# Six of twelve score tiles a pair transposed by PE, and a plan that holds an engine for an operation's time less its overlap with the next

## The chip, the cores and the metric

The kernel runs on one core of one Trainium2 chip. The metric is the device time of one execution in microseconds, as the median of several runs.

## The reference

Attention over buckets, then two feed-forward layers, all in float32. Both batches (2) and heads (8) have 768 tokens of 64 numbers.

```python
q_bucket = sum over 6 bits of ((q @ proj) > 0) * 2**bit      # k_bucket alike
scores = where(q_bucket[:, None] == k_bucket[None, :], q @ k.T / 8, -1e9)
attn = exp(scores - max); attn = attn / (sum + 1e-9)
x = (attn @ v), heads side by side                           # 1536 x 512
h = x @ w_in;  g = maximum(0.01 * h, h);            x = g @ w_out    # 512 -> 2048 -> 512
h = x @ w_in2; g = max(h, 0) + alpha * min(h, 0);   out = g @ w_out2
```

The weights come as float64 and are turned to float32 on the chip by integer operations.

## The kernel before, in words

**Attention.** The 16 heads go in eight pairs (two heads of one batch, index `i`; the head is `j`). Of a pair there are twelve score tiles of 128 query rows by 768 keys: two halves `f` of the rows, in each six tiles `m`, whose row block `t` and head `j` stand in `TILES`. `score` (from L694) makes one: PE multiplies (L710) into one of two PSUM tiles of the ring `s_ps`; DVE copies it to one of five buffers of the ring `s` and takes the row minimum (L717); ACT takes the exponential with its row sum (L720). Then the tile must be turned over, keys onto partitions, for the product with v. There are two ways, and `HI_ON` and `LO_ON` (for the last pair `HI_LAST` and `LO_LAST`) say for each of the twelve tiles which is taken:

- `T`: PE transposes the float32 tile in two groups of three (L736), each through the one PSUM bank of the ring `p_ps`, and ACT copies each group to `pt` (L741, `FP` = 0 leaves ACT alone).
- else: the tile is split in two float16 halves. With `P` in `LO_ON`, POOL scales it (L413, called at L752) and subtracts for the low half (L416); with `D`, DVE makes the low half in one operation (L760). The high half is a cast (L754) by ACT, or also by POOL where the plan may choose: before, for the `D` tiles alone; with `FH` = 1 for both. When both heads of a row block are there, one DMA transpose from SP's queue turns them over (L766).

`pv` multiplies with v for a half: six steps of PE, in each six float16 products over the row blocks that were split (L807) and two float32 products for each block that came by `T` (L816; each stands in the trace as two records). `kept` counts the split blocks of a half. Then DVE multiplies by the reciprocal sum (L823). For the next pair k and q are loaded, split (L416 on POOL, `split_qk`), turned over (L539) and their bucket bits made (L582, L591).

**Feed-forward.** Both layers run over four groups of 512 hidden columns and the two batches. `convert` (from L965) turns a float64 weight piece to float32 by five operations (ACT L993, DVE L995, L999, L1002, L1005) and to a scaled float16 pair; the common scale of a group comes out of `power` (from L924), with a PE product with ones (L950) that spreads a maximum over the partitions, in a PSUM bank of `b_banks`, and a DVE read of it (L954). Every product is three float16 products (L1164 to L1166). `leaky` makes the activation, `y_group` (from L1267) the second product and its sum (L1298).

**The order of the work.** Nothing is ordered by hand: each step is an operation of `Plan`, with one or more `ways` (engine, cost in us, for DVE whether it needs the port that it shares with POOL in the model, and for a DMA its time on the queue), a `claim` that orders the ring buffers, and a `turn` that orders operations that are ready at one time. `Plan.first` makes a list schedule, `late` and `early` push it back and forth (`PASSES`, for six values of `PATIENCE`), and the order that ends first by the costs is written out for each engine. `Lines` holds each engine from an operation's start to its cost's end; `hop` is the delay between engines, 0 on the same one. In this model a DMA transpose takes SP for 3.7 and the DMA line for 4.0 us.

Of the kernel before, what the change touches and what calls it, by code (L numbers as in the profile page):

```python
# [27 lines left out]
F64_MAX = 122879.9921875  # L28

TILES = ((0, 0), (2, 0), (0, 1), (1, 0), (2, 1), (1, 1))  # L30
HI_ON = "ATPATPATPATA"
LO_ON = "P-DP-DP-DP-D"

HI_LAST = "ATPATPATATTT"
LO_LAST = "P-DP-DP-D---"
SB = 5
FT, FP, FR, FH, FV, FB = 0, 0, 1, 0, 0, 0


HOP, HOP_PE, LANDING = 0.12, 0.29, 1.6  # L40
PATIENCE, PASSES = (0.05, 0.1, 0.15, 0.2, 0.25, 0.3), 7


LEAN_V, LEAN_X, LEAN_W = 0.0,0.0,0.0

X_LEAD, CONV = 30, (2, 5, 19, 6)
START, XAT = 10.0, (1, 9)

# [48 lines left out]
    __slots__ = ("ways", "claim", "reads", "writes", "deps", "left", "users", "n", "start", "done", "way", "turn", "lean")  # L97


def hop(one, other):  # L100

    return 0.0 if one[0] == other[0] != "SP" else HOP_PE if one[0] == "PE" else HOP


class Line:
# [25 lines left out]
class Lines(dict):  # L131
# [9 lines left out]
    def soonest(self, op, last=False):  # L141

        best = None
        for k, way in enumerate(op.ways):
            eng, dur, port, _ = way
            at = 0.0
            for u, full in op.deps.items():
                at = max(at, u.done + hop(u.ways[u.way], way) if full else u.start)
            lines, x = self.of(way), 0.0
            if last:  # L150
                at = max([at] + [line.ends[-1] for line in lines if line.ends])
            else:
                while (then := max(line.early(at, dur) for line in lines)) > at + 1e-9:
                    at = then
            done = at + dur
            if eng == "SP":
                x = at + dur / 2
                x = max([x] + self["DMA"].ends[-1:]) if last else self["DMA"].early(x, port)
                done = x + port + LANDING
            cost = done - (op.lean if eng == "POOL" else 0.0)  # L160
            if best is None or cost < best[0]:
                best = cost, (at, done, x, k)
        return best[1]

    def latest(self, way, start, done):
        eng, dur, port, _ = way
        if eng == "SP":
            x = self["DMA"].late(done - LANDING, port)
            return self["SP"].late(min(start, x - dur / 2) + dur, dur), x + port + LANDING, x
        at, lines = min(start, done - dur), self.of(way)  # L170
        while (then := min(line.late(at + dur, dur) for line in lines)) < at - 1e-9:
            at = then
        return at, at + dur, 0.0

    def put(self, way, at, x):
        for line in self.of(way):
            line.put(at, way[1])
        if way[0] == "SP":
            self["DMA"].put(x, way[2])

# [125 lines left out]
def lsh_attention_ffn_kernel(  # L306
# [13 lines left out]
    nc = tc.nc  # L320
    B, H, S, D = q.shape
# [15 lines left out]
    NP = len(pairs)  # L337
    N = 12 * NP

    ctx.enter_context(tc.manual_schedule())  # L340
    plan = Plan()
# [55 lines left out]
    def vec(dur, fn, port=False):  # L397
        return "DVE", dur, port, fn
# [4 lines left out]
    def gps(dur, fn):  # L403
        return "POOL", dur, 0, fn
# [270 lines left out]
        )  # L675

    def engines(i):
        return (HI_ON, LO_ON) if i < NP - 1 else (HI_LAST, LO_LAST)

    def kept(i, f):  # L680

# [233 lines left out]
    def bank(ring):  # L915
        return Bank(ring.new([128, 1, HALF], F32, "h"), 0)
# [7 lines left out]
    def power(claim, cols_, most, most_use, scale_, scale_use, extra=None, reads=(), writes=(), wide=False, to=2.0**13):  # L924

        dg_ = bt_r.new([128, S], F32, "dg")
        dg = lambda: dg_.t.bitcast(F32R)[:, 0:128]
        mx = mx_r.new([128, 1], F32, "mx")
        ps = b_banks.take() if claim >= N + 2 else bank(t_ps)
        buf, n = cols_  # L930

        def diag():
            nc.vector.tensor_reduce(out=mx.t, in_=buf.t[:, 0:n], axis=AX.X, op=ALU.max)
            if not wide:
                nc.vector.tensor_single_scalar(
                    mx.t.bitcast(I32), mx.t.bitcast(I32), EXPONENT, op=ALU.bitwise_and
                )
                return
            low, high = buf.t[:, 0:1].bitcast(I32), mx.t.bitcast(I32)
            nc.vector.tensor_scalar(  # L940
                out=low, in0=high, scalar1=3, scalar2=0x3F800000, op0=ALU.logical_shift_left,
                op1=ALU.bitwise_and,
            )
            nc.vector.scalar_tensor_tensor(
                out=high, in0=high, scalar=0x40000000, in1=low, op0=ALU.bitwise_and, op1=ALU.bitwise_or
            )

        plan.add(claim, vec(0.5 if wide else 0.35, diag), [buf], [mx, buf] if wide else [mx])
        plan.add(claim, diagonal(dg, mx), [mx, ident], [dg_])
        plan.add(claim, pe(0.2, lambda: nc.tensor.matmul(  # L950
            ps.ap(128), lhsT=ones.t, rhs=dg(), start=True, stop=True)), [dg_, ones], [ps.use()])

        def scales():
            nc.vector.tensor_reduce(out=most(), in_=ps.ap(128), axis=AX.X, op=ALU.max)  # L954
            nc.vector.tensor_scalar_max(most(), most(), V_MIN)
            nc.vector.tensor_single_scalar(
                scale_().bitcast(I32), most().bitcast(I32), EXPONENT, op=ALU.bitwise_xor
            )
            nc.vector.tensor_scalar_mul(scale_(), scale_(), to)  # L959
            if extra:  # L960
                extra()

        plan.add(claim, vec(0.95 if extra else 0.8, scales), [ps.use(), *reads], [most_use, scale_use, *writes])

    def convert(n, claim, step, early=None):  # L965

        l, fq, nm = groups[n]
        mw = mw_r.new([128, FQ], F32, "mw")
# [2 lines left out]
        for k in range(FQ // per):  # L971
# [5 lines left out]
            for a, one in enumerate(each):  # L977
# [14 lines left out]
            w = per * DM  # L992
            plan.add(first, act(0.16 + w * 0.00098, lambda m=m, high=high: nc.scalar.activation(  # L993
                out=m.ap(F32), in_=high().bitcast(F32), func=AF.Abs)), [r.use()], [m.use()], turn=now)
            plan.add(first, vec(0.24 + w * 0.00052, lambda m=m, k=k: nc.vector.tensor_scalar(  # L995
                out=m.ap(F32), in0=m.ap(F32), scalar1=F64_MAX, scalar2=F64_MIN, op0=ALU.min,
                op1=ALU.max, accum_out=mw.t[:, k:k + 1]), True),
                [m.use()], [m.use(), col(mw, k)], turn=now)
            plan.add(first, vec(0.18 + w * 0.00052, lambda m=m: nc.vector.tensor_scalar(  # L999
                out=m.ap(I32), in0=m.ap(I32), scalar1=3, scalar2=0x3FFFFFFF,  # L1000
                op0=ALU.logical_shift_left, op1=ALU.bitwise_and), True), [m.use()], [m.use()], turn=now)
            plan.add(first, vec(0.19 + w * 0.00104, lambda m=m, low=low: nc.vector.scalar_tensor_tensor(  # L1002
                out=low(), in0=low(), scalar=29, in1=m.ap(I32), op0=ALU.logical_shift_right,
                op1=ALU.bitwise_or), True), [m.use(), r.use()], [r.use()], turn=now)
            plan.add(first, vec(0.19 + w * 0.00104, lambda low=low, high=high: nc.vector.scalar_tensor_tensor(  # L1005
                out=low(), in0=high(), scalar=-0x40000000, in1=low(), op0=ALU.bitwise_and,
                op1=ALU.bitwise_or), True), [r.use()], [r.use()], turn=now)

# [37 lines left out]
        for p in range(0, FQ, 2):  # L1046
# [16 lines left out]
            for out_, x, y, op, to, frm in (  # L1063
                (s1, a21, a22, ALU.add, r1, r2), (s3, a11, a21, ALU.subtract, r2, r1),
                (s2, s1, a11, ALU.subtract, r1, r1), (s4, a12, s2, ALU.subtract, r2, r1),
            ):
                def add(out_=out_, x=x, y=y, op=op, eng=None):
                    eng.tensor_tensor(out=out_(), in0=x(), in1=y(), op=op)
                plan.add(claim, [
                    vec(0.37, lambda add=add: add(eng=nc.vector), True),  # L1070
                    gps(0.7, lambda add=add: add(eng=nc.gpsimd))], [r1.use(), r2.use()], [to.use()])
            halves(claim, wide, lambda r1=r1: r1.ap(F32).rearrange("p (d two) -> p two d", two=2),
                   [r1.use()], c, c_use, 2)
            halves(claim, thin, lambda r2=r2: r2.ap(F32).rearrange("p (d two) -> p two d", two=2)[:, :, DM // 2:],
# [70 lines left out]
    def x_sum(b, nm, claim, turn):  # L1145
        (x, xu), (y, yu) = (x_part(b, a) for a in {
            "T3": ("B22", "B12"), "T1": ("B12", "B11"), "T2": ("B22", "B11"), "T4": ("B21", "B11")}[nm])
        o, ou = (y, yu) if nm == "T2" else (x, xu)
        op = ALU.add if nm == "T2" else ALU.subtract
        plan.add(claim, [vec(0.95, lambda: nc.vector.tensor_tensor(out=o(), in0=x(), in1=y(), op=op), True),  # L1150
                         gps(1.9, lambda: nc.gpsimd.tensor_tensor(out=o(), in0=x(), in1=y(), op=op))],
                 [xu, yu], [ou], turn)

# [29 lines left out]
    def leaky(u, f, n, claim, src, src_use, own=None):  # L1183
# [7 lines left out]
        else:  # L1191
            plan.add(claim, act(0.58, lambda: nc.scalar.activation(
                out=g.ap(F32), in_=src(), func=AF.Copy, scale=low_by.t[:, f:f + 1])),
                [src_use, low_by], [g.use()])
            plan.add(claim, vec(0.56, lambda: nc.vector.scalar_tensor_tensor(  # L1195
                out=g.ap(F32), in0=src(), scalar=high_by.t[:, f:f + 1], in1=g.ap(F32),
                op0=ALU.mult, op1=ALU.max), own is not None), [src_use, g.use(), high_by], [g.use()])
        plan.add(claim, act(0.51, lambda: nc.scalar.copy(out=gh.ap(), in_=g.ap(F32))),  # L1198
# [221 lines left out]
```

## Time and profile before

| | before |
|---|---|
| runs | 756.92, 761.02, 762.53 us; median 761.02 |
| profiled execution | 758.8 us, of which the span is 757.0 |
| busy in the span | PE 705.5, DVE 624.1, ACT 487.7, POOL 312.9 us |
| mean granted TensorE clock | 0.983 of full speed |
| DMA | 77.89 MB, 39.3% of 16 engines' span on the main queue |

Times of rows are microseconds from the span's start. PE is TensorE's products, PEld its weight loads, DVE VectorE, ACT ScalarE, POOL GpSimd, SP SyncE with the DMA queue. PE's ends are modelled and overlap, so the pace of PE is read from starts.

### The profile page before, as it was taken

The page shows a single profiled execution, that of the slowest core. Times are in us where ns is not written, and L with a number is a line of the kernel's source. Part 1 is how long each engine was busy: PE and PEld are TensorE (multiplying, and loading weights), DVE is VectorE, ACT ScalarE, POOL GpSimd, SP SyncE. Part 2 cuts the span into 40 slices and gives each one's busy share as a digit, 9 for nine tenths or more (in the row PEclk, how much of TensorE's full clock was granted, in tenths as well). Part 3 has the DMA queues.
Part 4 walks back from the last instruction along what each step waited for, and adds up shares of the span by engine and source line. Part 5 has one row for each costly group of instructions (what it writes and reads, how often), then busy time and mean ns, then how long its engine had stood idle before and what let it go on. Part 6 is the DMA issues. An engine that isn't in the chain of part 4 may idle for free.

```text
span 757.0 us, 12700 instructions
## 1 busy us (share of the span) xinstructions
PE 705.5 (93%) x4727; PEld 448.2 (59%) x4727; DVE 624.1 (82%) x1105; ACT 487.7 (64%) x903; POOL 312.9 (41%) x316
## 2 busy tenths in 40 slices
PE   7789978988987799999999999999999999999997
PEld 5577767877876556655565556555454555555553
DVE  6889898788899987879888886999997989986442
ACT  5887878897889676666656545565675764654340
POOL 2776757866564052213332532324043324333220
PEclk9989999999999899999999999999999999999999
DMA  7597997988757430331322313120311212100012
GB/s 208 126 197 166 194 197 168 221 173 177 157 129 145 171 103 9 111 113 41 106 77 74 95 56 111 34 78 1 112 52 60 84 59 82 55 1 2 15 55 98
DMA packets 131214, 77.89 MB, mean 103 GB/s; under 512 B 100864, under 2 KB 123392, under 8 KB 131152
## 3 DMA queue, kind: packets, MB, share of 16 engines
q1 hardware_dynamic: 131152, 77.08, 39.3%
q8 instruction: 37, 0.61, 0.3%
q14 instruction: 25, 0.20, 0.1%
HBM read 43.00 MB, written 3.15 MB: 61 GB/s over the span
## 4 chain that ended last, share of the span: by engine, by line
PE 66%; DVE 25%; ACT 4%; issue 3%; POOL 1%; DMA 0%; SPq 0%; DVEq 0%; POOLq 0%
PE y L1164 10%; PE y L1166 10%; PE y L1165 10%; PE sc L710 7%; PE h L1164 6%; PE h L1166 6%; PE h L1165 6%; DVE ff L1089 4%; PE o L807 3%; DVE s L717 3%; PE pp L736 2%; PE o L816 2%; DVE ff L995 2%; DVE ff L1002 2%; DVE hl L760 2%
## 5 line engine op out<-in xcount | busy, mean ns | idle before, releaser
L416 POOL TENSOR_TENSOR ff<-ff 128x384 f16<-128x384 f32 x128 | 138.4, 1095 | 282.2 <-ACT ff L1198 241.9
L1164 PE MATMUL y<-ff 128*128 128x384 f16 (+1 forms) x496 | 171.9, 347 | 9.4 <-DVE ff L1209 2.8
L1166 PE MATMUL y<-ff 128*128 128x384 f16 (+1 forms) x496 | 171.8, 346 | 0.0
L1165 PE MATMUL y<-ff 128*128 128x384 f16 (+1 forms) x496 | 171.8, 346 | 0.0
L1164 PE MATMUL h<-ff 128*128 128x384 f16 x416 | 136.3, 328 | 2.9 <-ACT ff L1087 2.8
L1165 PEld LDWEIGHTS <-ff 128*128 128x128 f16 x912 | 89.4, 98 | 81.1 <-issue 14.9
L1166 PE MATMUL h<-ff 128*128 128x384 f16 x416 | 136.2, 327 | 0.7 <-DVE ff L1089 0.7
L1165 PE MATMUL h<-ff 128*128 128x384 f16 x416 | 136.1, 327 | 0.0
L1164 PEld LDWEIGHTS <-ff 128*128 128x128 f16 x912 | 89.3, 98 | 71.3 <-ACT ff L1087 2.9
L1166 PEld LDWEIGHTS <-ff 128*128 128x128 f16 x912 | 89.3, 98 | 70.6 <-DVE ff L1089 1.1
L717 DVE TENSOR_SCALAR_CACHE_REDUCE s<-sc 128x768 f32<-128x768 f32 x96 | 89.6, 951 | 19.1 <-PE sc L710 13.1
L720 ACT ACTIVATE s<-s,mn 128x768 f32<-128x768 f32 x96 | 89.6, 935 | 13.2 <-DVE s L717 12.5
L1298 DVE SCALAR_TENSOR_TENSOR x<-y,back,x 128x384 f32<-128x384 f32 (+1 forms) x84 | 56.3, 670 | 37.9 <-PE y L1166 35.1
L1198 ACT CAST ff<-ff 128x384 f16<-128x384 f32 x128 | 64.6, 510 | 23.2 <-DVE ff L1195 21.2
L1205 ACT COPY ff<-h 128x384 f32<-128x384 f32 x72 | 34.1, 477 | 56.1 <-PE h L1166 55.0
L710 PE MATMUL sc<-ka,qa 128*128 128x384 f32 x192 | 59.8, 394 | 8.8 <-DVE s L717 8.6
L416 POOL TENSOR_TENSOR hl<-s,hl 128x768 f16<-128x768 f32 x31 | 53.1, 1712 | 30.0 <-ACT hl L754 29.9
L710 PE MATMUL sc<-kb,qb 76*128 76x384 f32 x192 | 51.7, 350 | 0.2 <-ACT kb L613 0.2
L1089 DVE SCALAR_TENSOR_TENSOR ff<-ff,by 128x512 f16<-128x512 f32 (+2 forms) x54 | 48.1, 919 | 3.3 <-ACT ff L1087 3.1
L1087 ACT ACTIVATE ff<-ff,by 128x512 f16<-128x512 f32 (+2 forms) x54 | 43.7, 863 | 10.0 <-DVE by L959 8.2
L807 PE MATMUL o<-pt,vb 128*64 128x256 f16 (+1 forms) x576 | 48.2, 276 | 0.0
L1002 DVE SCALAR_TENSOR_TENSOR ff<-ff 128x1024 int32<-128x1024 int32 (+1 forms) x36 | 45.9, 1275 | 0.8
(142 smaller groups left out, 1207.2 us busy)
## 6 DMA issues: line engine op xcount, KB each, us to landing
ff<-in_moe_w_in_dram SPq DMA_DIRECT2D x32, 512.0 KB
ff<-in_moe_w_out_dram SPq DMA_DIRECT2D x32, 512.0 KB
v<-in_v_dram SPq DMA_DIRECT2D x8, 384.0 KB
out_dram<-x SPq DMA_DIRECT2D x12, 256.0 KB
k<-in_k_dram SPq DMA_DIRECT2D x7, 384.0 KB
q<-in_q_dram SPq DMA_DIRECT2D x7, 384.0 KB
kb<-ka SPq DMA_DIRECT2D x14, 192.0 KB
qb<-qa SPq DMA_DIRECT2D x14, 192.0 KB
```

Of the source, the lines that this page charges most:

```text
L416: nc.gpsimd.tensor_tensor(out=o, in0=a, in1=b, op=ALU.subtract)
L710: nc.tensor.matmul(sc.t[:, h, 0:HALF], lhsT=o[a].t[0:rows, row:row + 128], rhs=o[b].t[0:rows, h * HALF:h * HALF + HALF], start=(n == 0), s ...
L717: plan.add(g, vec(1.03, lambda: nc.vector.tensor_scalar(out=s.t.rearrange("p (a b) -> p a b", a=2), in0=sc.t[:, :, 0:HALF], scalar1=FILL, ...
L720: plan.add(g, act(1.12, lambda: nc.scalar.activation(out=s.t, in_=s.t, func=AF.Exp, scale=-1.0, bias=mn.t[:, 0:1], accum_out=sm.t[:, t, j: ...
L807: nc.tensor.matmul(ps.t[64 * j:64 * j + 64, 0:split], lhsT=vb.t[:, piece, j, c, :], rhs=narrow(pt, i, f)[:, 2 * T * j + o + c], start=(c + ...
L1002: plan.add(first, vec(0.19 + w * 0.00104, lambda m=m, low=low: nc.vector.scalar_tensor_tensor(out=low(), in0=low(), scalar=29, in1=m.ap(I3 ...
L1089: plan.add(claim, vec(0.2 + w * 0.00108, lambda: nc.vector.scalar_tensor_tensor(out=part(lo), in0=src(), scalar=c(), in1=part(hi), op0=ALU ...
L1164: nc.tensor.matmul(ps, lhsT=lh[0], rhs=rh[0], start=first, stop=False, skip_group_check=skip)
L1165: nc.tensor.matmul(ps, lhsT=lh[0], rhs=rh[1], start=False, stop=False, skip_group_check=skip)
L1166: nc.tensor.matmul(ps, lhsT=lh[1], rhs=rh[0], start=False, stop=last, skip_group_check=skip)
L1198: plan.add(claim, act(0.51, lambda: nc.scalar.copy(out=gh.ap(), in_=g.ap(F32))), [g.use()], [gh.use()])
L1298: plan.add(claim, vec(0.69 if l else 0.56, lambda: nc.vector.scalar_tensor_tensor(out=a(), in0=ps.ap(w), scalar=c(), in1=a(), op0=ALU.mult ...
```

## The change

Six of twelve tiles of every pair are `T` (places 1, 3, 4, 5, 7 and 10; before 1, 4, 7 and 10, and in the last pair 1, 4, 7, 9, 10 and 11), the last pair has no pattern of its own, and POOL may take the high half of every split tile. The plan holds an engine for a cost less an overlap (`held`), and an operation may follow another on its engine by that much earlier. Costs of DVE and POOL operations are set anew, the converters' operations other than DMAs take a `turn` that is later by 6 (`LAG`), and `power` takes a fixed bank: 0 for weights, 1 for the others. No instruction of the feed-forward is added or left out.

```diff
-HI_ON = "ATPATPATPATA"
-LO_ON = "P-DP-DP-DP-D"
-
-HI_LAST = "ATPATPATATTT"
-LO_LAST = "P-DP-DP-D---"
+HI_ON = "ATATTTATPATP"
+LO_ON = "P-D---P-DP-D"
 SB = 5
-FT, FP, FR, FH, FV, FB = 0, 0, 1, 0, 0, 0
+FT, FP, FR, FH, FV, FB = 0, 0, 1, 1, 0, 0
...
+OVERLAP = {"ACT": 0.1, "DVE": 0.08, "POOL": 0.04}
...
+LAG = 6
...
+def held(way):
+
+    return max(way[1] - OVERLAP.get(way[0], 0.0), 0.05)
+
+
 def hop(one, other):

-    return 0.0 if one[0] == other[0] != "SP" else HOP_PE if one[0] == "PE" else HOP
+    if one[0] == other[0] != "SP":
+        return held(one) - one[1]
+    return HOP_PE if one[0] == "PE" else HOP
...
-                while (then := max(line.early(at, dur) for line in lines)) > at + 1e-9:
+                while (then := max(line.early(at, use) for line in lines)) > at + 1e-9:
...
-        while (then := min(line.late(at + dur, dur) for line in lines)) < at - 1e-9:
+        at, lines, use = min(start, done - dur), self.of(way), held(way)
+        while (then := min(line.late(at + use, use) for line in lines)) < at - 1e-9:
...
-            line.put(at, way[1])
+            line.put(at, held(way))
...
     def engines(i):
-        return (HI_ON, LO_ON) if i < NP - 1 else (HI_LAST, LO_LAST)
+        return HI_ON, LO_ON
...
-        ps = b_banks.take() if claim >= N + 2 else bank(t_ps)
+        ps = b_banks.got[0 if wide else 1] if claim >= N + 2 else bank(t_ps)
...
-        plan.add(claim, vec(0.95 if extra else 0.8, scales), [ps.use(), *reads], [most_use, scale_use, *writes])
-
-    def convert(n, claim, step, early=None):
+        plan.add(claim, vec(1.2 if extra else 1.0, scales), [ps.use(), *reads], [most_use, scale_use, *writes])
+
+    def convert(n, *args):
+        first = len(plan.ops)
+        convert_now(n, *args)
+        for op in plan.ops[first:]:
+            if n > 1 and op.ways[0][0] != "SP":
+                op.turn += LAG
+
+    def convert_now(n, claim, step, early=None):
...
-            plan.add(first, vec(0.24 + w * 0.00052, lambda m=m, k=k: nc.vector.tensor_scalar(
+            plan.add(first, vec(0.2 + w * 0.00105, lambda m=m, k=k: nc.vector.tensor_scalar(
...
-            plan.add(first, vec(0.18 + w * 0.00052, lambda m=m: nc.vector.tensor_scalar(
+            plan.add(first, vec(0.13 + w * 0.00071, lambda m=m: nc.vector.tensor_scalar(
...
-            plan.add(first, vec(0.19 + w * 0.00104, lambda m=m, low=low: nc.vector.scalar_tensor_tensor(
+            plan.add(first, vec(0.13 + w * 0.00123, lambda m=m, low=low: nc.vector.scalar_tensor_tensor(
...
-            plan.add(first, vec(0.19 + w * 0.00104, lambda low=low, high=high: nc.vector.scalar_tensor_tensor(
+            plan.add(first, vec(0.13 + w * 0.0012, lambda low=low, high=high: nc.vector.scalar_tensor_tensor(
...
-                    vec(0.37, lambda add=add: add(eng=nc.vector), True),
-                    gps(0.7, lambda add=add: add(eng=nc.gpsimd))], [r1.use(), r2.use()], [to.use()])
+                    vec(0.47, lambda add=add: add(eng=nc.vector), True),
+                    gps(0.8, lambda add=add: add(eng=nc.gpsimd))], [r1.use(), r2.use()], [to.use()])
...
-        plan.add(claim, [vec(0.95, lambda: nc.vector.tensor_tensor(out=o(), in0=x(), in1=y(), op=op), True),
+        plan.add(claim, [vec(1.1, lambda: nc.vector.tensor_tensor(out=o(), in0=x(), in1=y(), op=op), True),
...
-            plan.add(claim, vec(0.56, lambda: nc.vector.scalar_tensor_tensor(
+            plan.add(claim, vec(0.6 if own is None else 0.68, lambda: nc.vector.scalar_tensor_tensor(
```

## Rows read from the trace of the kernel before

**Rows 1.** Stages: length, busy us (instructions) of each engine, PE clock, DMA share, GB/s.
```profile
0.00:236.00 236.00, 209.09 (x1807) 167.83 (x1807) 198.93 (x402) 188.87 (x387) 152.80 (x160) 0.96 0.80 175
40.00:220.00 180.00, 164.44 (x1511) 134.21 (x1511) 153.91 (x302) 147.59 (x303) 121.17 (x116) 0.96 0.87 185
236.00:257.00 21.00, 13.22 (x167) 10.81 (x167) 20.16 (x37) 14.89 (x27) 2.20 (x3) 0.92 0.45 142
257.00:744.00 487.00, 474.02 (x2712) 265.64 (x2713) 401.98 (x664) 283.89 (x491) 157.88 (x154) 1.00 0.20 66
```

**Rows 2.** One line's instructions: the score tiles on DVE, durations, first and last start.
```profile
L717 DVE TENSOR_SCALAR_CACHE_REDUCE s<-sc x96: 914/951/959, 15.4 to 236.4; 128x768 f32<-128x768 f32 x96
```

**Rows 3.** Groups by shape, 0 to 265 us: count, busy us, mean ns, idle before.
```profile
L416 POOL TENSOR_TENSOR hl<-s,hl 128x768 f16<-128x768 f32 x31 | 53.1, 1712 | 30.0 <-ACT hl L754 29.9
...
L760 DVE SCALAR_TENSOR_TENSOR hl<-s,hl 128x768 f16<-128x768 f32 x31 | 42.0, 1354 | 0.4 <-ACT hl L754 0.2
...
L754 ACT ACTIVATE hl<-s 128x768 f16<-128x768 f32 x47 | 39.2, 840 | 0.8 <-POOL s L413 0.3 <-DMA pt<-hl 0.2
...
L736 PE MATMUL pp<-ident,s 128*128 128x128 f32 x204 | 36.4, 288 | 9.4 <-ACT s L720 5.0 <-ACT pt L741 4.4
L741 ACT COPY pt<-pp 128x384 f32<-128x384 f32 x68 | 32.2, 473 | 18.6 <-PE pp L736 18.2
...
L413 POOL TENSOR_SCALAR s<-s 128x768 f32<-128x768 f32 x31 | 27.9, 901 | 20.2 <-ACT s L720 20.0
```

**Rows 4.** Order in time on PE: start, length; transposes, and steps of the product with v.
```profile
101.61 0.55 PE L736 MATMUL pp<-ident,s 128*128 128x128 f32 x3
...
101.99 0.49 PE L539 MATMUL tp<-ident,qn 128*128 128x128 f32 x3
...
109.33 0.49 PE L807 MATMUL o<-pt,vb 128*64 128x256 f16 x6
...
109.87 0.49 PE L807 MATMUL o<-pt,vb 128*64 128x256 f16 x6
...
250.83 0.33 PE L807 MATMUL o<-pt,vb 128*64 128x128 f16 x6
...
251.43 0.33 PE L807 MATMUL o<-pt,vb 128*64 128x128 f16 x6
```

**Rows 5.** Order in time on PE, the last transposes of the last pair.
```profile
243.05 0.55 PE L736 MATMUL pp<-ident,s 128*128 128x128 f32 x3
244.22 0.55 PE L736 MATMUL pp<-ident,s 128*128 128x128 f32 x3 [0.63 <-ACT pt L741]
246.25 0.55 PE L736 MATMUL pp<-ident,s 128*128 128x128 f32 x3 [1.48 <-ACT pt L741]
```

**Rows 6.** Order in time, DVE and ACT, around 103 us: start, length.
```profile
102.19 0.96 DVE L717 TENSOR_SCALAR_CACHE_REDUCE s<-sc 128x768 f32<-128x768 f32 x1
...
103.07 0.08 DVE L717 DVE_READ_ACCUMULATOR s<-sc 128x1 f32 x1
...
103.19 0.94 ACT L720 ACTIVATE s<-s,mn 128x768 f32<-128x768 f32 x1
...
104.03 0.18 ACT L720 ACTIVATION_READ_ACCUMULATOR s<-s,mn 128x1 f32 x1
```

**Rows 7.** One line's instructions: DVE's low halves and SP's DMA transposes, ns least, median, most.
```profile
L760 DVE SCALAR_TENSOR_TENSOR hl<-s,hl x31: 946/1185/2414, 24.8 to 237.2; 128x768 f16<-128x768 f32 x31
...
L766 SPq DMA_TRANSPOSE pt<-hl x31: 2983/3303/6177, 26.3 to 238.4; - x31
```

**Rows 8.** Groups by shape, 265 to 757 us: the first clamp of a wide weight piece.
```profile
L995 DVE TENSOR_SCALAR_CACHE_REDUCE ff<-ff 128x1024 f32<-128x1024 f32 x28 | 33.9, 1209 | 3.2 <-ACT ff L993 3.2
```

**Rows 9.** Waits of PE, 265 to 757 us: us in total, times, longest us.
```profile
PE y L1164 <- DVE ff L1209: 2.8, 4, 1.0
PE y L1164 <- DVE biggest L954: 2.4, 5, 0.8
PE y L1164 <- DVE x L1298: 2.4, 5, 0.7
```

More of the change, by code (lines that the diff above doesn't have):

```diff
@@ L145, in soonest @@
             eng, dur, port, _ = way
+            use = held(way)
             at = 0.0
@@ L169, in latest @@
             return self["SP"].late(min(start, x - dur / 2) + dur, dur), x + port + LANDING, x
-        at, lines = min(start, done - dur), self.of(way)
-        while (then := min(line.late(at + dur, dur) for line in lines)) < at - 1e-9:
+        at, lines, use = min(start, done - dur), self.of(way), held(way)
+        while (then := min(line.late(at + use, use) for line in lines)) < at - 1e-9:
             at = then
```

## The prediction

> **What bounds the kernel now.** I read the busy time by stage first, then the pace of the score tiles, then the groups by shape, then the order in time at three places, and the waits of the last stage at the end. The stages show three different limits [rows 1]. In the feed-forward (257 to 744 us) PE is busy 474.0 of 487.0 us and so is the bound: 13.0 us of idle, 2.7%. In the attention (0 to 236 us) no engine is the bound by itself: PE 209.1, DVE 198.9, ACT 188.9 and POOL 152.8 us of 236, with PE idle for 26.9 us (11.4%); in its steady part, 40 to 220 us, PE is idle 15.6 of 180 us (8.6%) and the DMA engines are 0.87 busy. Between the two (236 to 257 us) DVE is busy 20.2 of 21 us while PE does 13.2. So what the change can win lies in 26.9 us of the attention, about 8 us of the crossing and 13 us of the feed-forward, and what it can lose lies where PE, already the busiest engine, gets more. The first score tile is taken by DVE at 15.4 us and the ninety-sixth at 236.4 [rows 2], which is 221.0/95 = 2.33 us a tile, 27.9 us a pair.
>
> **The change part by part.** (1) Six transposed tiles a pair instead of four. The last pair has six in both kernels, so seven pairs change, by two tiles each. Counts of before and after: transpose groups on PE 68 to 96 (L736, three transposes each), their copies on ACT 68 to 96 (L741), DVE low halves 31 to 24 (L760), POOL scalings 31 to 24 (L413), POOL low halves 31 to 24 (L416), DMA transposes 31 to 24, high halves 62 to 48.
>
> What goes, by the mean of each [rows 3]: DVE 7 x 1.354 = 9.5 us; POOL 7 x (0.901 + 1.712) = 18.3 us; of the 14 high halves that go, seven were on ACT for certain, 7 x 0.840 = 5.9 us. What comes: ACT 28 x 0.473 = 13.2 us, so ACT gains 7.3 us net at most, and less where the plan now gives high halves to POOL. On PE a transpose group was issued 0.38 us before the next work (101.61 to 101.99) where nothing held it, so 28 x 0.38 = 10.6 us; six steps a pair of the product with v have two whole tiles instead of one, and a step's pace goes from 0.54 us (109.33 to 109.87) to 0.60 (250.83 to 251.43) [rows 4], 42 x 0.06 = 2.5 us. PE's attention work goes from 209.1 to 222.2 us.
>
> How much of these 13.1 us shows depends on how well PE's idle is closed, and no row shows it for the new mix. From both sides: with the idle share of the feed-forward, 2.7%, the attention would take 222.2/0.973 = 228.4 us (-7.6); with the share of its own steady part, 8.6%, 243.1 us (+7.1); with its present 11.4%, 250.8 us (+14.8). It breaks even at 236.0, an idle share of 5.8%. I take 4%, 231.5 us, so -4.5. I go to the side of the feed-forward's row because everything that PE waits for here gets lighter (DVE 4.8%, POOL 12%, a quarter of the DMA transposes), and because of (3).
>
> The three neighbouring T tiles of a first half (places 3, 4 and 5) pass one PSUM bank in six turns, each a PE group and an ACT copy. The trace has two paces for such turns: 1.17 us (243.05 to 244.22) and 2.03 us (244.22 to 246.25), the second behind other work of ACT [rows 5]. Six turns at 1.17 are 7.0 us, and three tiles arrive in 3 x 2.33 = 7.0 us. So this is free at the good pace only; ACT's copies are what is late next.
>
> (2) The last pair ends on a tile for the DMA, where before its last three tiles were PE's. Before, the last score was taken at 236.4 us [rows 2] and the last step of the product began at 251.43 [rows 4]. After, behind the same moment come the score 0.95, the exponential 0.94 [rows 6], a high half 0.84 [rows 3], a low half of 0.95 at its least [rows 7], a DMA transpose of 3.3 us (its longest 6.2; that is the queue's instruction, the landing may be later) and six steps of 0.54: 10.2 to 13.1 us against 15.6. It can win some us or lose as many if ACT and DVE are late, as both also make the inputs of the feed-forward there. I take 0, between -7.8 (all of PE's idle in the crossing) and +3 (the longest DMA twice over).
>
> (3) The plan holds ACT 0.10, DVE 0.08 and POOL 0.04 us less per operation. The rows bear the first two out: the exponential that starts at 103.19 lasts 0.94 us and the next instruction starts at 104.03, 0.10 before its end; DVE's at 102.19 lasts 0.96 and the next starts at 103.07, 0.08 before its end [rows 6]. Over the 387 ACT and 402 DVE instructions of the attention [rows 1] the old plan held the engines for up to 38.7 and 32.2 us that they did not need. This costs no instruction; it changes the order alone. It is why I take 4% rather than the break-even.
>
> DVE's low halves take 0.946 us at the least, 1.185 in the middle and 2.414 at most [rows 7], for one shape. The Trainium skill has a rule on this that speaks against part (1): in SBUF — State Buffer, "SBUF: two separate sides", GpSimd and a VectorE operation with two SBUF inputs take their shared ports as a lock for a whole instruction. By it the new freedom to put a high half on POOL beside POOL's own low half (FH = 1) would make DVE's remaining low halves wait as before, and nothing beyond the 9.5 us is saved on DVE; by the rows alone POOL's lighter load would bring their mean down towards 0.946, at most 24 x 0.41 = 9.8 us more. The sum above takes none of these 9.8 us. A spread like this one agrees with a lock; the row alone does not show what each slow one stood beside.
>
> (4) New DVE costs in the converters, a later turn for them (LAG), and a fixed PSUM bank for each scale product. They change the order in the feed-forward. The old cost of the first clamp of a wide piece is 0.24 + 1024 x 0.00052 = 0.77 us; the trace has 1.209 [rows 8], and with an accumulator read of 0.08 [rows 6] 1.29, and the new cost is 1.28. The neighbouring edits of costs have the same answer. What it can win is what PE waits for DVE: 2.8 + 2.4 + 2.4 = 7.6 us [rows 9]. What it can lose: the fixed bank makes each of the 15 scale products of this stage wait for DVE's read of it; at the longest such wait, 0.8 us, that is 12.0 against today's 2.4, so +9.6. I take -2, nearer to today's row than to either end, since PE is at 97% already.
>
> The sum: -4.5 + 0 - 2 = -6.5 us. The profiled execution took 758.8 us (span 757.0 and 1.8 around it), so it would be 752.3. The median of the runs shown is 761.0, 0.3% more; on that it is 754.5. I forecast 753, between the two.
>
> **The rivals.** *A, slower: the one transposition bank.* If the six turns go at the middle of their two paces, 1.60 us, three T tiles take 9.6 us where 7.0 are to be had; 2.6 us a pair, seven pairs, 18.2 us: 771. It decides from 1.17 us a turn. For it: ACT's copies already stand in a queue with exponentials of 0.94 us, and the present row of PE groups has 9.4 us of idle before it [rows 3]. Against: five score buffers let the plan spread the turns over other tiles, and twelve turns at 1.60 are 19.2 of 27.9 us.
>
> *B, no change.* The relief of DVE and POOL just pays for PE's 13.1 us: the attention ends at its break-even of 5.8% idle and the feed-forward as before, 759 to 761, say 760. For it: PE is the busiest of the engines already [rows 1]. The same comes out if the new order does not do what it says, because the actual pace is not set by the plan's clock.
>
> *C, a large gain.* The attention reaches the feed-forward's idle share (-7.6), the crossing loses 5 of its 7.8 us of idle, the feed-forward 5 of its 7.6: -17.6, from the median's side 743, from the profile's 741, say 742.
>
> **How the numbers follow.** The forecast has 0.45, its own range 748 to 759; A 0.15; B 0.25; C 0.15. The range of 742 to 769 leaves out half of C and the upper part of A, about 0.2. A measurement of this kernel tells about 1% from no change, that is 753.4 and 768.6 around the median. Faster: C and 0.27 of the forecast, 0.42. Within 1%: B and 0.18 of the forecast, 0.43. Slower: A, 0.15.
>
> **What would show it.** Right: 96 transpose groups and 24 DVE low halves; score tiles at 2.25 to 2.30 us; PE at 95 to 97% of the attention; the last score tile near 232 us; the feed-forward at 484 to 486 us. Rival A: ACT's copies named as what PE's groups wait for, with turns over 1.2 us. B: last score again near 236 us, PE's idle about 14 us. C: last score near 228 us and the first product of the feed-forward within 16 us of it. I am wrong if PE's work in the attention grows by much other than 13 us, or if the feed-forward moves by over 8 us either way.

## The result and the profile after

The changed kernel takes 751.42 us (750.42 to 751.94, four runs) where the kernel before takes 759.63 in the same comparison: a ratio of 0.989, 95% interval 0.9847 to 0.9932. The profiled execution has a span of 750.2 us, 6.8 less than before. The forecast was 753 us, with -6.5 on the profiled execution. Times are medians of runs in the faster of two states that the chip shows; one run of e4 below, 769.1 us at a granted clock of 0.932, is left out for it.

The stages of the changed kernel, in the columns of [rows 1] (length, busy us of PE, PEld, DVE, ACT, POOL, granted PE clock, DMA share, GB/s). The first row ends at the last score tile, the third at the first product of the feed-forward:

```profile
0.00:230.60 230.60, 221.06 (x2149) 179.22 (x2149) 187.04 (x394) 187.72 (x402) 146.98 (x159) 0.99 0.69 156
40.00:215.00 175.00, 173.09 (x1778) 142.48 (x1778) 144.47 (x313) 145.70 (x316) 120.81 (x119) 1.00 0.73 160
230.60:244.20 13.60, 4.17 (x17) 2.50 (x17) 13.22 (x30) 9.72 (x18) 1.31 (x2) 0.65 0.78 212
244.20:750.20 506.00, 488.05 (x2813) 273.17 (x2813) 404.92 (x680) 284.82 (x493) 151.71 (x143) 0.99 0.20 66
```

In the steady part PE is busy 173.1 of 175.0 us, 98.9%, where [rows 1] had 91.4%. Until the last score tile PE is idle 9.5 of 230.6 us (4.1%); before it was 27.3 of 236.4. DMA's share fell from 0.80 to 0.69. The score tiles on DVE answer to [rows 2]:

```profile
L724 DVE TENSOR_SCALAR_CACHE_REDUCE s<-sc x96: 910/956/959, 17.8 to 230.6; 128x768 f32<-128x768 f32 x96
```

That is 212.8/95 = 2.24 us a tile against 2.33, and the last one 5.8 us earlier. Behind it come 519.6 us to the end of the span against 520.6. So 5.8 of the 6.8 us come up to the last score. The two stretches do not hold quite the same work, though. In the changed kernel the product with v of the last pair's first half, six steps at 0.61 us, stands ahead of the last score; before, it began behind it. First and last step after, then the first step before:

```profile
226.31 0.36 PE L814 MATMUL o<-pt,vb 128*64 128x128 f16 x6 [0.27 <-DVE x L830]
...
229.34 0.36 PE L814 MATMUL o<-pt,vb 128*64 128x128 f16 x6
...
238.46 0.52 PE L807 MATMUL o<-pt,vb 128*64 128x256 f16 x6
```

The groups that answer to [rows 3], 0 to 265 us:

```profile
L743 PE MATMUL pp<-ident,s 128*128 128x128 f32 x288 | 51.3, 288 | 6.9 <-ACT pt L748 6.5
...
L748 ACT COPY pt<-pp 128x384 f32<-128x384 f32 x96 | 45.7, 476 | 27.7 <-PE pp L743 27.2
L423 POOL TENSOR_TENSOR hl<-s,hl 128x768 f16<-128x768 f32 x24 | 42.6, 1777 | 2.7 <-ACT hl L761 1.1
...
L767 DVE SCALAR_TENSOR_TENSOR hl<-s,hl 128x768 f16<-128x768 f32 x24 | 24.7, 1029 | 2.7 <-ACT hl L761 2.7
...
L420 POOL TENSOR_SCALAR hl<-s 128x768 f16<-128x768 f32 x28 | 23.3, 831 | 8.8 <-ACT s L727 7.2
L420 POOL TENSOR_SCALAR s<-s 128x768 f32<-128x768 f32 x24 | 22.7, 946 | 34.2 <-ACT s L727 34.0
```

The counts are the forecast ones: 288 transposes (96 groups), 96 copies, 24 low halves on DVE. The copies wait for PE (27.2 us, 18.2 before) far more than PE for them (6.5 us, 4.4 before): PE is the late one, and by as much as before, 0.28 us a copy against 0.27. DVE's low halves take 1.029 us on average instead of 1.354, so DVE lost 42.0 - 24.7 = 17.3 us of them, not the 9.5 of the sum.

### The profile page after: what moved, and what is told of

Read it like the earlier page. It is cut to its first block, busy times and chain, and to the rows that moved or that the text cites. A ratio compares the mean times of both kernels' runs of the same rounds, so it can differ in the third digit from the quotient of the medians.

```text
span 750.2 us, 13172 instructions
## 1 busy us (share of the span) xinstructions
PE 713.3 (95%) x4979; PEld 454.9 (61%) x4979; DVE 605.2 (81%) x1102; ACT 482.3 (64%) x911; POOL 300.0 (40%) x304
## 4 chain that ended last, share of the span: by engine, by line
PE 75%; DVE 17%; ACT 5%; issue 2%; DMA 0%; SPq 0%; DVEq 0%; ACTq 0%
PE y L1178 10%; PE y L1180 10%; PE y L1179 10%; PE h L1178 7%; PE h L1180 7%; PE h L1179 7%; PE sc L717 7%; PE pp L743 4%; PE o L814 4%; PE o L823 4%; DVE ff L1103 3%; PE tp L546 2%; ACT s L727 2%; PE bp L589 2%; DVE ff L1019 2%
## 5 line engine op out<-in xcount | busy, mean ns | idle before, releaser
L423 POOL TENSOR_TENSOR ff<-ff 128x384 f16<-128x384 f32 x128 | 137.9, 1093 | 319.3 <-ACT ff L1212 247.6
L724 DVE TENSOR_SCALAR_CACHE_REDUCE s<-sc 128x768 f32<-128x768 f32 x96 | 90.2, 953 | 17.4 <-PE sc L717 13.5
L748 ACT COPY pt<-pp 128x384 f32<-128x384 f32 x96 | 45.7, 476 | 27.7 <-PE pp L743 27.2
L717 PE MATMUL sc<-ka,qa 128*128 128x384 f32 x192 | 57.4, 380 | 1.8 <-DVE s L724 1.4
L743 PE MATMUL pp<-ident,s 128*128 128x128 f32 x288 | 51.3, 288 | 6.9 <-ACT pt L748 6.5
L823 PE MATMUL o<-pt,v 128*64 128x128 f32 x576 | 47.6, 273 | 0.0
```

Of the source, the lines that this page charges most:

```text
L423: nc.gpsimd.tensor_tensor(out=o, in0=a, in1=b, op=ALU.subtract)
L717: nc.tensor.matmul(sc.t[:, h, 0:HALF], lhsT=o[a].t[0:rows, row:row + 128], rhs=o[b].t[0:rows, h * HALF:h * HALF + HALF], start=(n == 0), s ...
L724: plan.add(g, vec(1.03, lambda: nc.vector.tensor_scalar(out=s.t.rearrange("p (a b) -> p a b", a=2), in0=sc.t[:, :, 0:HALF], scalar1=FILL, ...
L743: nc.tensor.transpose(ps.t[:, c], s.t[:, k0:k0 + 128], ident.t)
L823: nc.tensor.matmul(ps.t[64 * j:64 * j + 64, t * 128:t * 128 + 128], lhsT=v32.t[:, j, c, :], rhs=whole(pt, t)[:, T * j + c], start=False, s ...
```

## The experiments

Each kernel is the one before with a part of the change, or with work added, and was timed beside the kernel before. The table has the median times, and of one profile each the start of the last score tile, PE's busy time and its idle until then, the granted clock of that stretch and what the span has behind that tile. The profiles of e2 and e3 are of the slowest of their four runs (780.9 and 773.9 us). In after, e1 and e4 the half product named above stands ahead of the last score, as do five of its six steps in e10 and not quite two in e8; in the others it stands behind. That alone moves some 3.6 us between the columns.

| kernel | T tiles | time us | ratio, 95% interval | last score | PE busy | PE idle | clock | rest of span |
|---|---|---|---|---|---|---|---|---|
| before | 4 | 759.6 | | 236.4 | 209.1 | 27.3 | 0.96 | 520.6 |
| e2 overlap alone | 4 | 775.4 | 1.0198, 1.0128 to 1.0267 | 249.4 | 218.3 | 31.1 | 0.94 | 529.7 |
| e3 costs, LAG, bank alone | 4 | 768.9 | 1.0112, 1.0042 to 1.0181 | 253.4 | 218.8 | 34.6 | 0.93 | 518.7 |
| e5 delay 0.13 | 4 | 755.9 | 0.9949, 0.9921 to 0.9977 | 231.3 | 204.3 | 27.0 | 1.00 | 520.1 |
| after | 6 | 751.4 | 0.989, 0.9847 to 0.9932 | 230.6 | 221.1 | 9.5 | 0.99 | 519.6 |
| e1 pattern and FH | 6 | 749.9 | 0.9856, 0.9811 to 0.9901 | 232.4 | 219.6 | 12.8 | 1.00 | 516.8 |
| e7 pattern alone | 6 | 748.5 | 0.9853, 0.9791 to 0.9914 | 228.2 | 216.4 | 11.8 | 0.99 | 520.5 |
| e4 pattern, FH, overlap | 6 | 752.1 | 0.9888, 0.9842 to 0.9933 | 235.9 | 220.1 | 15.8 | 0.99 | 514.2 |
| e6 e1 with delay 0.13 | 6 | 756.9 | 0.9963, 0.9932 to 0.9995 | 234.3 | 219.8 | 14.5 | 0.98 | 522.9 |
| e8 e1 and DVE work | 6 | 754.7 | 0.9937, 0.9906 to 0.9969 | 229.2 | 217.6 | 11.6 | 1.00 | 523.3 |
| e9 e1, DVE and POOL work | 6 | 752.1 | 0.9912, 0.9879 to 0.9945 | 230.2 | 214.8 | 15.4 | 0.99 | 519.2 |
| e10 e1 and DMA loads | 6 | 767.5 | 1.0113, 1.0075 to 1.0151 | 247.6 | 226.3 | 21.3 | 1.00 | 517.6 |
| e12 e10, loads hardly planned | 6 | 761.0 | 1.0004, 0.9978 to 1.0029 | 239.5 | 223.5 | 16.0 | 0.99 | 520.9 |
| e11 six and four in turn | 5 | 749.4 | 0.9883, 0.9835 to 0.9930 | 227.9 | 210.5 | 17.4 | 0.99 | 520.1 |

**The parts of the change, e1 to e4.** e1 has the first two hunks of the diff and `engines`; e2 `OVERLAP`, `held`, `hop` and `Lines`; e3 the costs, `LAG` and the fixed bank; e4 e1 and e2 together.

> Only the tile pattern and POOL's freedom for the high halves (FH); old plan model, old costs. Theory, both together: the 12 us that PE gets more stay mostly on the path because the old order holds ACT and DVE too long; PE idle about 8% of the attention, the last score tile taken at 234 to 239 us, time 757 to 763 us. Rival, the relief alone: DVE, POOL and the DMA were what PE waited for; the last score at 230 to 232 us, time 751 to 754 us.

> Only the plan's overlap (held and hop); four T tiles, old costs. Theory, both together: PE has no more work, the order is a little better; the last score at 233 to 236 us, time 756 to 760 us. Rival, the order alone: the last score at 229 to 232 us with PE at about 209 us busy, time 751 to 754 us.

> Only the new costs, LAG and the fixed bank of the scale products; old pattern, old plan model. Theory: the attention stays at 236 us for the last score, from there to the end 518 to 523 us (520.6 before), time 757 to 762 us. Rival, the costs alone make the gain by a better feed-forward: from the last score to the end under 515 us, time under 755 us.

> Pattern, FH and overlap; old costs, no LAG, old banks. Theory: all of the gain is here; the last score at 229 to 232 us, PE idle about 4% before it, time 750 to 754 us. Rival, the costs are needed: the last score as in the changed kernel but from there to the end over 523 us, time 755 us or more.

The rival of e1 holds in time: the pattern with FH gives the whole gain, 749.9 us, on the old plan model (its last score, 232.4 us, is just past the rival's 230 to 232). The theory, that the gain needs both, fell in e1, and more so in e2: with four tiles the overlap makes the kernel 2.0% slower, and the new costs make it 1.1% slower. Both lose in the attention (13.0 and 17.0 us at the last score, in profiles of their slowest runs), e2 also 9.1 us behind it; my expectation for e3, an attention that stays as it was, missed. e4 shows no gain of the overlap with six tiles either.

**Is that the order, or the work? e5 and e6.** Edit of both, on the kernel before and on e1:

```diff
-HOP, HOP_PE, LANDING = 0.12, 0.29, 1.6
+HOP, HOP_PE, LANDING = 0.13, 0.29, 1.6
```

> The kernel before with one number of the plan moved, the delay between engines from 0.12 to 0.13 us: four T tiles, another order, no other work. Theory, after the single parts: with four T tiles no engine is the bound, the time hangs on the order, and the order before was a good one among many; the last score at 240 to 255 us, time 763 to 780 us. Rival: the overlap and the new costs are worse for reasons of their own, and a mere change of order does nothing; last score at 235 to 238 us, time 757 to 762 us.

> The six-tile pattern with FH and otherwise the kernel before, with the same 0.13 us. Theory: with six T tiles PE is the bound of the attention, so another order changes little; the last score at 229 to 236 us, PE idle 4 to 7% before it, time 748 to 754 us. Rival, the pattern alone was one lucky order: time 757 us or more.

Another order of the same work moves the time by -3.7 us with four tiles and by +7.0 with six. My expectation for e5 missed (the order before was not a specially good one), and so did its rival; e6 came out between its two cases: the last score and idle of the theory, a time above it. What this settles is the grain: a difference of some 7 us between two orders of the same work says nothing of their parts. The four kernels with four tiles have 755.9 to 775.4 us (mean 765.0), the five with six and no added work 748.5 to 756.9 (mean 751.8): the gain of the pattern, as a mean over orders, stands out of this; a gain or loss of the plan's edits with six tiles (after against e1, 1.5 us) does not. Pair by pair the pattern's gain is not steady: -9.7 us on the plan before (e1), -23.3 with the overlap (e4 against e2), but +1.0 with the delay of 0.13 (e6 against e5). What all nine kernels share is PE's idle until the last score: 27.0 to 34.6 us with four tiles, 9.5 to 15.8 with six. The last pair's new pattern was not timed apart from the others.

e5 shows one thing more beside the kernel before. The stretch to its last score tile:

```profile
0.00:231.30 231.30, 204.32 (x1807) 160.11 (x1807) 193.25 (x398) 189.83 (x391) 159.77 (x162) 1.00 0.81 179
```

The same 1807 products, idle 27.0 against 27.3 us, and 4.8 us less busy: nearly all of the 5.1 us are PE's own pace, at a granted clock of 1.00 against 0.96. In the kernel before, the clock in steps of 2 us around 40 us (columns as in [rows 1]):

```profile
37.00:39.00 2.00, 0.55 (x3) 0.31 (x3) 2.00 (x6) 0.71 (x2) 2.00 (x3) 1.00 0.00 0
39.00:41.00 2.00, 1.95 (x7) 1.79 (x7) 1.14 (x3) 1.87 (x3) 2.00 (x2) 0.50 0.86 191
41.00:43.00 2.00, 1.22 (x6) 0.68 (x5) 2.00 (x5) 1.26 (x3) 1.92 (x3) 0.50 1.01 226
43.00:45.00 2.00, 2.00 (x10) 2.00 (x11) 2.00 (x2) 1.38 (x4) 0.78 (x1) 0.50 0.29 51
45.00:47.00 2.00, 2.00 (x12) 1.87 (x10) 0.67 (x2) 2.00 (x6) 1.02 (x1) 0.79 0.75 211
```

PE had been busy 0.55 of 2 us; then it was granted 0.50, its lower level of 1.2 GHz, for some 6 us, and the clock rose again while PE worked without a gap (from 43 us on). So this idle stretch was paid twice. The kernel before has four such stretches from 14 us to its last score (the others from 18, 184 and 212 us on), e5 none, though its idle is as long and it has steps of 2 us with no more than 0.73 us of work: not every gap is followed by a lower clock, and these runs do not show what decides. e2 and e3, at mean clocks of 0.94 and 0.93, paid most: PE is busy 14.0 and 14.5 us longer than in e5 with nearly the same products (1813 and 1808). The clock also goes with the spread of one kernel's runs: the kernel before took 756.5 us at a mean clock of 0.988 and 766.9 us at 0.971.

This bears on the gain. Of the 14 profiles, e5, e1, e8 and e10 have no lowered clock from 14 us to the last score. The spans of e5 and e1, four tiles against six, are 751.4 and 749.2 us: 2.2 us apart, where their medians are 6.0 apart and the profiles before and after 6.8. In these two profiles e1 has 14.2 us less idle and 15.3 us more work (the half product among it). So where the clock stays up the pattern wins little more than it costs, and much of the measured gain goes with a clock that falls less often. With one profile of each this is a reading, not a proof; and the 4.8 us are an estimate of the clock's price, as PE's busy time also grows where products stand further apart (226.3 us in e10, with fewer products than e1's 219.6 and the clock at 1.00).

**POOL's freedom, e7.** e1 with FH = 0.

> The six-tile pattern alone, without POOL's freedom for the high halves of the P tiles (FH = 0); otherwise the kernel before. Theory: the freedom is worth little, ACT has slack; time 749 to 755 us. Rival, the freedom carries ACT's new copies: time 756 us or more, with ACT over 195 us busy before the last score.

The theory holds: 748.5 us, just below its range, with ACT at 186.6 us before the last score. The freedom is not needed.

**Which relief closes PE's idle? e8 to e10 and e12.** Each gives back, for seven pairs, what two tiles a pair had taken from an engine, on a spare buffer that nothing uses; the outputs are not changed.

```diff
+            if m == 5 and i < NP - 1:
+                plan.add(g + 2, vec(1.02, lambda: nc.vector.scalar_tensor_tensor(
+                    out=spare.t, in0=s.t, scalar=1.0, in1=spare.t,
+                    op0=ALU.mult, op1=ALU.subtract), True), [s, spare], [spare])
+                plan.add(g + 2, gps(0.84, lambda: gmul(spare.t, s.t, 1.0)), [s], [spare])
+                plan.add(g + 2, gps(1.79, lambda: gsub(spare.t, s.t, spare.t)), [s, spare], [spare])
```

This is e9; e8 has its first operation alone; e10 has in its place three loads `dma(1.2, ...)` from q, and e12 the same with `dma(0.05, ...)`.

> Six-tile pattern with FH, and DVE is given one low-half operation a pair back (on a spare buffer, for seven pairs, its result not used). Theory, PE is now the bound: DVE has the room; the last score at 230 to 236 us, time 749 to 754 us. Rival, DVE's relief was the gain: time 755 to 761 us.

> Six-tile pattern with FH, and both engines get back about what two tiles a pair took from them: DVE one low-half operation, POOL one cast and one subtraction (on a spare buffer, seven pairs, results not used). Theory, PE's own work fills its idle and PE is the bound: DVE and POOL have the room; last score at 229 to 236 us, PE idle 10 to 16 us before it, time 749 to 757 us. Rival, the relief of POOL, with the port it shares with DVE, closed the idle: DVE's remaining low halves go back to 1.3 us or more, last score at 236 us or later, PE idle over 20 us, time 758 us or more.

> Six-tile pattern with FH, and SP's queue gets back about the time of a DMA transpose a pair (three loads of 192 KB into a spare buffer, seven pairs). Theory, PE is the bound: last score at 229 to 236 us, time 749 to 757 us. Rival, the DMA queue's relief closed PE's idle: DMA share 0.8 or more, last score at 236 us or later, PE idle over 20 us, time 758 us or more.

DVE and POOL had the room as far as the last score shows, 229.2 and 230.2 us. In time e9 is in the theory's range; e8, 754.7 us, lies between theory and rival, and both are inside the spread of orders, so a cost of a few us is not excluded. In e9 DVE's low halves stay at 1.095 us:

```profile
L765 DVE SCALAR_TENSOR_TENSOR hl<-s,hl 128x768 f16<-128x768 f32 x24 | 26.2, 1095 | 0.4 <-POOL hl L411 0.4
```

The loads are another matter: e10 is at 767.5 us, far out of that spread, with the last score tile at 247.6. Its rival wanted a DMA share of 0.8 and over 20 us of idle; the idle came (21.3), the share did not:

```profile
0.00:247.60 247.60, 226.34 (x2132) 174.99 (x2134) 200.26 (x404) 190.23 (x396) 139.26 (x151) 1.00 0.70 159
```

So the mean share does not explain it; single stretches are not excluded (1.02 from 100 to 120 us). Two things were left: the queue of SP, which the loads share with the transposes, and the plan's DMA line, whose time the loads fill again.

> The same 21 added loads as in e10, but the plan is told 0.05 us of the DMA line for each instead of 1.2. The chip moves the same bytes. Theory, the plan's own DMA line was full (in its costs 29.6 us a pair with four T tiles, 25.6 with six, 29.2 with six and the loads) and the order that it writes is stretched by it: last score at 229 to 237 us, time 749 to 758 us. Rival, the transfers themselves stand in the way on the queue or the engines: last score at 243 us or later, time 762 us or more.

e12 lies between the two, at 761.0 us. Told almost nothing of the loads, the plan writes an order that is 6.5 us faster than e10's, but still 11.1 slower than e1's, 7.1 of it by the last score and 4.1 behind, where e12 still has the half product to do. The 6.5 us are no more than a mere change of order moved above. Behind its last score PE has one long wait for a transpose of the last pair:

```profile
PE o L810 <- DMA pt<-hl: 8.2, 1, 8.2
```

The queue (SP's order in time) shows what that transpose stood behind: four weight loads, themselves behind a group of transposes that took SP 26.6 us, waits included.

```profile
218.06 26.62 SPq L769 DMA_TRANSPOSE pt<-hl  x4
244.85 0.46 SPq L408 DMA_DIRECT2D ff<-in_moe_w_in_dram  x1
245.36 1.45 SPq L408 DMA_DIRECT2D ff<-in_moe_w_out_dram  x3
246.92 7.56 SPq L769 DMA_TRANSPOSE pt<-hl  x1
```

But the fast e1, without added loads, has the same picture in its queue, so this does not tell the two apart:

```profile
204.32 26.61 SPq L763 DMA_TRANSPOSE pt<-hl  x4
232.30 0.39 SPq L407 DMA_DIRECT2D ff<-in_moe_w_in_dram  x1
232.75 1.56 SPq L407 DMA_DIRECT2D ff<-in_moe_w_out_dram  x3
234.75 7.78 SPq L763 DMA_TRANSPOSE pt<-hl  x1
```

Nor does PE wait much for transposes ahead of the last score: 1.5 us in e10, nothing in e12. DVE's low halves are slower in both, 1.398 and 1.294 us against 1.124 in e1. So, of the work given back, the loads alone cost time beyond the spread of orders; whether by SP's queue, by the plan's line or by the order that came of it, these runs do not show.

**Is PE now the bound? e11.** e7 with the old pattern in the odd pairs:

```diff
+HI_ODD = "ATPATPATPATA"
+LO_ODD = "P-DP-DP-DP-D"
...
-        return HI_ON, LO_ON
+        return (HI_ODD, LO_ODD) if i % 2 else (HI_ON, LO_ON)
```

> Six T tiles in the pairs of even number, four in the odd ones (FH = 0, otherwise the kernel before), to be held beside e7. Theory, PE is the bound with six: PE's work before the last score falls by about 8 us against e7, and part of it comes back as idle; last score at 224 to 230 us, time 744 to 750 us. Rival, PE has to be the bound in every pair to keep its clock and its idle closed: PE idle over 20 us, last score at 231 us or later, time 752 us or more.

The numbers lie in the theory's range (227.9 and 749.4 us), but not for its reason: PE's work fell by 5.9 us against e7 and its idle rose by 5.6, so nothing was won. PE at 95% of the attention is not a bound by itself here: with PE a little lighter the attention ended at the same time. e7, e1 and e11 have lower medians than the changed kernel, but their intervals overlap with its own.

## Why the prediction was right, and which reasons were not

- *The sum.* -6.5 us against -6.8 in the profiled executions. Its first term, -4.5 for the attention, measured -5.8; the other two, 0 and -2, together -1.0. That this came so near is in part luck: those two measured -7.0 (20.6 to 13.6 us) and +6.0 (500.0 to 506.0 us from the first product of the feed-forward to the end), and both -5.8 and -7.0 hold a product that changed its place.
- *PE's added work and its idle share.* I had 13.1 us and 4%; 12.0 us and 4.1% were measured. That the work agrees is luck, as four differences cancel. Until the last score 30 groups were added, not 28 (276 transposes against 186), and the half product of six steps: at my prices 0.8 and 3.6 us more, so 17.5. At a full clock 219.6 - 204.3 = 15.3 us were measured (e1 against e5, both at 1.00), 2.2 less than those prices. And the kernel before had some 4.8 us of PE's time in a lowered clock, the changed one 1.5 (against e1), which I did not price. e9, whose half product stands behind the last score as in e5, has 10.4 us more than e5, where my prices give 13.9. So 0.38 us for a group was not too little.

```profile
0.00:232.40 232.40, 219.59 (x2150) 176.70 (x2150) 190.32 (x390) 181.82 (x393) 155.08 (x168) 1.00 0.69 155
0.00:230.20 230.20, 214.75 (x2065) 174.62 (x2065) 189.06 (x397) 183.31 (x397) 161.41 (x171) 0.99 0.66 154
```

- *The reason for 4%.* Here the prediction failed: "It is why I take 4% rather than the break-even" rested on step (3), the overlap. The pattern without the overlap gives 748.5 and 749.9 us, and the overlap alone 775.4. The 38.7 us that the old plan held ACT too long counted every instruction; 93 of the 387 are reads of an accumulator, which are one operation of the plan with their exponential, so it was 29.4 at most. And holding ACT more truly did not make a better order. What stays is the other half of that reason, that what PE waits for gets lighter; and of DVE, POOL and DMA, which I named together, only added loads cost time beyond the spread of orders, by a way that stays open.

```profile
L720 ACT ACTIVATION_READ_ACCUMULATOR s<-s,mn 128x1 f32 x93 | 17.8, 192 | 0.0
```

- *DVE's low halves and the lock.* The rule of the Trainium skill (SBUF — State Buffer, "SBUF: two separate sides") spoke for no saving beyond the 9.5 us, should POOL take more high halves. POOL took 28 instead of 15, and DVE's mean still fell to 1.029 us, 17.3 us in all. That does not speak against the lock, since POOL's work fell as a whole (152.8 to 147.0 us); it shows that the bad case did not come. That the saving closed the gap is not borne out by e9, which gave the work back and kept the last score at 230.2 us.
- *The crossing.* I took 0. The first product of the feed-forward comes 13.6 us behind the last score instead of 20.6; but one half product of the last pair now stands ahead of the stretch and the other behind it, from 251.26 to about 254.6 us, where before both lay in it. The clock there was 0.65. What the crossing itself gained is not shown.
- *The feed-forward.* I took -2 for truer costs, and 484 to 486 us as the sign of it, from 487. This failed: from its first product to its last PE takes 501.6 us where it took 495.8, and the half product that now lies in it is only 3.4 of these 5.8. What PE waits for from DVE did not fall: 7.6 us before [rows 9], now 6.1 + 1.9 + 1.5 + 0.8 + 0.7 = 11.0. Nor do the truer costs show a gain beside e1 and e4, which have the old ones and the same half product ahead of the last score: behind it they have 516.8 and 514.2 us, the changed kernel 519.6.

```profile
PE y L1178 <- DVE ff L1223: 6.1, 9, 0.7
...
PE h L1178 <- DVE ff L1209: 1.9, 1, 1.9
PE y L1178 <- DVE biggest L961: 1.5, 4, 0.4
PE y L1178 <- DVE y_max L961: 0.8, 2, 0.4
PE y L1178 <- DVE x L1312: 0.7, 1, 0.7
```

- *The rivals.* A, the one transposition bank, did not decide: the plan spread the turns over other tiles (45.23, 47.62, 50.01 us and so on), and all 96 groups together waited 6.5 us for ACT's copies.

```profile
45.23 0.49 PE L743 MATMUL pp<-ident,s 128*128 128x128 f32 x3
...
47.62 0.49 PE L743 MATMUL pp<-ident,s 128*128 128x128 f32 x3
...
50.01 0.49 PE L743 MATMUL pp<-ident,s 128*128 128x128 f32 x3
```

B would have left PE's idle at 14 us and the last score at 236; C needed 228 and a shorter feed-forward; of its signs only the first product within 16 us of the last score came (13.6), for the reason above. e7 reached C's 228.2 us, and its rest of span stayed at 520.5.

## What to carry to other kernels

Where no engine is the bound, moving work onto the engine that is already the busiest can pay: its idle, 27 us, was the loss here, and every order with six tiles had less of it. What is won is only the idle less the added work, a few us, unless the clock falls less often as well. Before a gain is put down to one part of a planner's change, time that part alone, and time a mere change of order as well: here the latter moved the time by up to 7 us, and the plausible half of the change was worth nothing that shows. Before two stretches are compared, count the instructions in them: one product that changes its place can look like a gain. A truer cost in a plan is not a faster plan.

## What was not expected of the hardware

An idle stretch of PE can cost again in its clock: after 0.55 us of work in 2 us the granted clock stood at 0.50 for the next 6 us, and two kernels with the same products and the same idle until the last score differ by 4.8 us of busy time at mean clocks of 0.96 and 1.00. And with 21 loads of 192 KB in seven pairs, at a mean DMA share of 0.70 to 0.71, the kernel was 11 to 18 us slower, in another order.
